# The end of a two-stage kernel as steps of its written order, and the bias of the rest rows stored twice

## The chip, the cores and the metric

The kernel runs on one core of a Trainium2 chip. The metric is the device time of one execution in microseconds (us), the median of the runs taken; each profiled execution also has a span, from its first to its last instruction.

## The reference

All numbers are float32. Stage one is attention over 8 batches (b), 8 heads, 576 tokens and a head width of 64, with a learned bias on the relative position; stage two is a soft mixture of 8 experts with 4 slots each over all 4608 tokens of width 512.

```python
scores = q @ k.T / sqrt(64)
x = log1p(abs(i - j)) / log1p(max(i, 1))
bias = relu(x[..., None] @ w1 + b1) @ w2          # hidden 32, one column per head
attn = softmax(scores + bias) @ v
x = attn as [4608, 512]                           # heads side by side
logits = x @ phi                                  # 32 slots
slot_in = softmax(logits, axis=0).T @ x           # over all tokens
slot_out[e] = relu(slot_in[e] @ w1[e]) @ w2[e]    # 512 -> 1024 -> 512
out = softmax(logits, axis=1) @ slot_out
```

## The kernel before

The work is cut into steps, and one text, `ORDER` (lines 24 to 238, 2568 steps), gives the sequence in which all steps are issued. A step is written `name/unit`, with a `+` that picks the other engine or the other form, and `@` with the PSUM banks that it takes. Each engine, and the queue of SyncE (SP) that issues nearly every transfer, goes through its own instructions in that sequence, so a transfer that waits for its buffer holds all the transfers behind it.

Attention is 40 units: 16 for the first pair of heads (two passes over the 8 batches) and 8 for each of the other three pairs. A unit has score tiles p of 128 query rows: tiles 0 to 3 are rows of one batch, and tile 4 is the 64 rest rows (576 = 4 x 128 + 64) of two batches. Per tile: `S` makes the scores on TensorE (line 519 in quarters, with a `+`, or line 513), `t` adds the bias on VectorE and keeps the extreme (530), `e` is the exponential on ScalarE (538), `a`, `m` and `n` divide (545, 549, 432), `T` and `R` turn the tile (491), `c` and `cR` copy it out of PSUM (435). Per unit, `M` multiplies by v (625), `x` copies and `xs` stores; `lq` and `lv` load q, k and v two units ahead.

The bias is made in the first hundred us, beside the first units, by 36 jobs of 16 rows each: `f` (971, 973), `B` (983), `E` (991, 993), and `D` (999), which stores the rows to memory. Jobs 0 to 31 go to `bias_m`, 128 rows for each of tiles 0 to 3; jobs 32 to 35, the 64 rest rows, go to `bias_r`. `b0` to `b4` (load_bias, line 421) read them back for a pair of heads: `b0` to `b3` in one transfer of 128 rows, `b4`, in which the 64 rows are wanted twice, in two transfers of 64 rows.

From unit 32 on, each batch is folded into the mixture's state: `K`, `KR`, `L`, `D`, `W`, `Z` on TensorE, and for the output weights `C` (turned logits), `cA`, `cB`, `cC` (826 to 834, on VectorE but for the exponential, 838). The 64 weight tiles of 512 KB come in one fixed sequence: `w0` and `w1` steps fetch 23 of them during attention, the steps from `wbm0` to `wxk` fetch 24 into buffers that attention gives back, and `r0` to `r16` fetch the last 17, each into a buffer that the first layer has used up. The first layer is `F0` to `F7` (1065), then `H`, `U`, `V` (1079, 1081, 1087, 435), in two halves Q; `k0` and `k1` turn the output weights (1111, 1114), each after the `cC` of four batches.

Behind the last step of the order stands a piece written out by hand (lines 1194 to 1216): second(cg, Q) is the second layer (1138) for a quarter cg of the output columns and a half Q of the slots; keep_second, gather (1148) and keep_gathered bring the result to the layout that the last product needs; outputs (1170) makes 512 KB halves that put copies (one on ScalarE, one on VectorE) and stores at once on SP's queue (1176); outputs_rest (1182) and put_rest do the same for the rest rows.

Of the kernel before, what the change touches and what calls it, by code (L numbers as in the profile page):

```python
# [29 lines left out]
E8/-1 f22.3/-1 D12/-1 f16.3/-1 E19/-1 f18.2/-1+ f17.0/-1 f17.3/-1 f17.2/-1 B17/-1@0 E17/-1 D10/-1  # L30
f16.0/-1 f16.2/-1 B16/-1@4 f22.2/-1+ f21.0/-1 E16/-1 f18.3/-1+ D15/-1 f22.0/-1 f23.3/-1 f18.1/-1 D8/-1
f22.1/-1 B22/-1@6 D19/-1 f23.1/-1+ f20.3/-1 D17/-1 f5.2/-1 E22/-1 D16/-1 f18.0/-1 B18/-1@2 f20.2/-1
f21.2/-1 f23.2/-1 f23.0/-1 f21.1/-1 E18/-1+ f5.1/-1 f1.2/-1 B23/-1@0 f21.3/-1+ B21/-1@4 f20.1/-1+ f20.0/-1+
B20/-1@6 E23/-1+ f3.3/-1+ S1/0+@2,0 f3.0/-1 E21/-1 f4.0/-1 E20/-1+ f3.1/-1+ f0.3/-1 b1/-1 t1.0/0
t1.1/0 S1/1+@4,6 t1.1/1 f1.0/-1+ f1.3/-1+ D22/-1 f3.2/-1+ f5.0/-1 f0.2/-1 B1/-1@2 t1.0/1 B3/-1@0
f0.1/-1 f5.3/-1+ B5/-1@6 e1.1/0 E5/-1+ e1.0/0 a1/0 D18/-1 f0.0/-1+ m1/0 f4.3/-1 f2.1/-1
f2.0/-1 D23/-1 D21/-1 B0/-1@4 E0/-1+ f4.2/-1 D20/-1 b2/-1 E3/-1 E1/-1 f2.3/-1+ f4.1/-1
S2/0+@0,6 n1.0/0 t2.1/0 lq/2 f2.2/-1+ e1.1/1 n1.1/0 t2.0/0 T1/0@2 c1/0 e2.1/0 B2/-1@4
e2.0/0 E2/-1 B4/-1@2 f7.2/-1 E4/-1+ D4/-1 a2/0+ S2/1+@6,0 m2/0 lq/3 t2.0/1 e1.0/1
e2.0/1 t2.1/1 e2.1/1 S1/2@2,4 t1.0/2 n2.0/0 n2.1/0 T2/0@6 t1.1/2 c2/0 S2/2@0,2 a2/1+  # L40
# [1231 lines left out]
```

## Time and profile before

| | |
|---|---|
| three runs | 577.73, 579.60 and 580.16 us; median 579.60 us |
| the profiled execution | 582.73 us, span 580.7 us |
| busy | TensorE 544.7 us, ScalarE 439.9, VectorE 426.7, GpSimd 230.7 |
| memory traffic | 115.92 MB |

A busy time is the merged time of an engine's instructions in the span. "PE" is the matmul side of TensorE and "PEld" its weight load, which overlaps it. "Chain" is the chain of work that ended last, followed back from the last instruction. A DMA share of 1 means that all 16 transfer engines had work.

### The profile page before, as it was taken

The numbers are of one execution on the slowest core, as the hardware profiler recorded it, in microseconds if no ns is written. First come the engines' busy times: TensorE is split into PE (matmuls) and PEld (weight loads), VectorE is DVE, ScalarE is ACT, GpSimd is POOL, SyncE is SP. The second block draws the span as 40 slices with busy tenths as digits, with TensorE's granted clock in tenths as the row PEclk, the third lists the DMA queues.
The fourth block names the chain that finished last, engine by engine and source line by source line (L and its number), as shares of the span: only waits on it lengthen the run. The fifth ranks groups of instructions, "written<-read, shape, count | busy, mean of one in ns | idle before, by whom it ended". The sixth has DMA issues, their size and how long they took to land.

```text
span 580.7 us, 23472 instructions
## 1 busy us (share of the span) xinstructions
PE 544.7 (94%) x9871; PEld 368.4 (63%) x9871; DVE 426.7 (73%) x1177; ACT 439.9 (76%) x925; POOL 230.7 (40%) x373
## 2 busy tenths in 40 slices
...
GB/s 175 294 144 185 186 284 244 168 241 228 243 142 85 171 115 196 85 245 145 84 64 140 304 189 293 128 43 217 104 181 165 181 149 307 330 323 400 152 320 333
DMA packets 46040, 115.92 MB, mean 200 GB/s; under 512 B 5488, under 2 KB 9712, under 8 KB 45936
## 3 DMA queue, kind: packets, MB, share of 16 engines
...
q10 hardware_dynamic: 144, 0.29, 0.1%
...
## 4 chain that ended last, share of the span: by engine, by line
PE 71%; DVE 11%; DMA 7%; POOL 4%; issue 3%; ACT 3%; SPq 1%; DVEq 0%; POOLq 0%; ACTq 0%
PE ps L625 18%; PE ps L519 14%; PE ps L491 14%; PE ps L513 7%; PE ps L983 5%; DVE y L530 4%; POOL y L432 3%; PE ps L1138 3%; DMA qk<-in_qk_dram 3%; PE ps L1065 3%; DVE f L973 2%; PE ps L705 2%; DMA xo<-xs 1%; PE ps L847 1%; DVE at L435 1%
## 5 line engine op out<-in xcount | busy, mean ns | idle before, releaser
L432 POOL TENSOR_SCALAR y<-y,sm 128x576 f32<-128x576 f32 x288 | 212.0, 751 | 148.0 <-DVE sm L549 91.8
L538 ACT ACTIVATE y<-y,mn 128x576 f32<-128x576 f32 x288 | 220.6, 769 | 18.1 <-DVE mn L530 12.9
L530 DVE CUSTOM_DVE_ANT_0 y<-ps,bm 128x576 f32<-128x576 f32 x256 | 185.4, 752 | 48.9 <-PE ps L519 30.6
L625 PE MATMUL ps<-at,v 64*64 64x288 f32 (+2 forms) x2880 | 163.6, 357 | 0.1
L435 ACT COPY at<-ps 128x1024 f32<-128x1024 f32 (+2 forms) x136 | 109.4, 819 | 34.3 <-PE ps L491 31.0
L519 PE MATMUL ps<-qk 64*64 64x512 f32 (+1 forms) x1600 | 124.1, 409 | 2.8 <-DVE mn L530 1.7
L625 PEld LDWEIGHTS ps<-at,v 64*64 64x64 f32 x2880 | 102.3, 133 | 24.3 <-DVE mn L530 0.2
L491 PE MATMUL ps<-ident,y 64*128 64x64 f32 x2592 | 107.7, 227 | 6.4 <-DVE mn L530 1.8
L491 PEld LDWEIGHTS ps<-ident,y 64*128 64x128 f32 x2592 | 93.9, 139 | 25.9 <-POOL y L432 9.8
L519 PEld LDWEIGHTS ps<-qk 64*64 64x64 f32 x1600 | 70.0, 132 | 62.8 <-issue 41.7
L435 DVE COPY at<-ps 128x1024 f32<-128x1024 f32 (+2 forms) x88 | 73.0, 841 | 4.7 <-PE ps L491 3.9
L513 PE MATMUL ps<-qk 64*128 64x64 f32 (+1 forms) x352 | 58.8, 436 | 0.3 <-DVE at L435 0.2
L545 POOL TENSOR_SCALAR sm<-sm 128x2 f32<-128x2 f32 x64 | 14.2, 221 | 104.5 <-ACT y L538 101.9
L538 ACT ACTIVATION_READ_ACCUMULATOR y<-y,mn 128x1 f32 x288 | 54.9, 190 | 0.0
L513 PEld LDWEIGHTS ps<-qk 64*128 64x128 f32 x352 | 39.2, 187 | 16.6 <-issue 13.0
L973 DVE TENSOR_SCALAR f<-tabs,scl,nb 128x512 f32<-128x512 f32 (+17 forms) x95 | 46.6, 547 | 1.0 <-DMA bias_m<-e 0.7
L983 PE MATMUL ps<-f,wbd 128*32 128x79 f32 (+47 forms) x640 | 41.5, 390 | 3.9 <-DVE f L973 2.5
L971 ACT ACTIVATE f<-tabs,cols,scl 128x432 f32<-128x432 f32 (+17 forms) x49 | 34.5, 752 | 3.0 <-DVE scl L335 1.8
L530 DVE CUSTOM_DVE_ANT_0 y<-ps,br 128x576 f32<-128x576 f32 x32 | 23.2, 754 | 14.9 <-PE ps L519 7.6
L983 PEld LDWEIGHTS ps<-f,wbd 128*32 128x32 f32 x640 | 20.0, 109 | 22.1 <-issue 9.5
L549 DVE RECIPROCAL sm<-sm 128x2 f32<-128x2 f32 x144 | 22.7, 162 | 10.9 <-POOL sm L545 8.2
L435 ACT COPY xts<-ps 128x576 f32<-128x576 f32 (+2 forms) x31 | 16.8, 541 | 13.8 <-PE ps L625 12.0
...
## 6 DMA issues: line engine op xcount, KB each, us to landing
wt<-in_moe_w_dram SPq DMA_DIRECT2D x62, 512.0 KB, 6.9
qk<-in_qk_dram SPq DMA_DIRECT2D x32, 576.0 KB, 4.6
v<-in_v_dram SPq DMA_DIRECT2D x40, 288.0 KB, 4.6
bias_m<-e SPq DMA_DIRECT2D x32, 295.5 KB, 3.8
bm<-bias_m SPq DMA_DIRECT2D x16, 576.0 KB, 5.4
out_dram<-ob SPq DMA_DIRECT2D x16, 512.0 KB, 4.9
...
xs<-xts SPq DMA_DIRECT2D x16, 288.0 KB, 5.3
```

The source lines that it names most:

```text
L432: nc.gpsimd.tensor_scalar(out=out, in0=y, scalar1=r, scalar2=1.0, op0=ALU.mult, op1=ALU.mult)
L435: (nc.vector.tensor_copy if eng else nc.scalar.copy)(out=out, in_=in_)
L491: nc.tensor.matmul(out, src[rs], ident[rs, rs], is_transpose=True, start=True, stop=True, tile_position=(64 * r, 0))
L513: nc.tensor.matmul(pss[hh].t[:, n, 0:w], x[rs, S + QP[p]:S + QP[p] + P], x[rs, ks], start=True, stop=True, tile_position=(64 * hh, 0))
L519: nc.tensor.matmul(pss[hh].t[64 * r:64 * r + 64, n, 0:w], x[rs, q0:q0 + 64], x[rs, ks], start=True, stop=True, tile_position=(64 * hh, 64 ...
L530: nc.vector.tensor_tensor_reduce(out=d["y", p][:, :, hh], in0=blocks(d["ps", p][hh].read().rearrange("a n j -> a (n j)")[:, 0:S]), in1=blo ...
L538: nc.scalar.activation(out=y, in_=y, func=AF.Exp, bias=d["mn", p][:, hh:hh + 1], scale=-1.0, accum_out=d["sm", p][:, hh:hh + 1])
L549: nc.vector.reciprocal(out=r, in_=r)
L625: nc.tensor.matmul(d["po"].t[64 * c:64 * c + 64, hh, 0:n], d["v"][rs, 64 * k:64 * k + 64], at[0][rs, k, c, cs], start=k == 0, stop=k == 8, ...
L971: nc.scalar.activation(out=f, in_=tabs[:, 0:n], func=AF.Relu, bias=cols[:, 1:2], scale=sc)
L973: nc.vector.tensor_scalar(out=f, in0=tabs[:, 0:n], scalar1=sc, scalar2=nb1[:, 0:1], op0=ALU.mult, op1=ALU.max)
L983: nc.tensor.matmul(pb.t[32 * t:32 * t + 32, a // 512, a % 512:a % 512 + c1 - c0], wbd, x, start=True, stop=True, tile_position=(0, 32 * t))
```

## The change

The hand-written piece is gone. Each of its calls is a step of the order now, with its copy and its store apart (`s` second, `so` keep_second, `g` gather, `ss` keep_gathered, `o` outputs, `p` copy, `P` store, `X`, `px` and `PX` for the rest rows), so that the order has 2644 steps, and they stand among the others: `s0.0` comes behind `F7` and ahead of the second half's `H`, `U`, `V`; `k1` comes behind all four of `s0.0`, `s1.0`, `s0.1` and `s1.1`; `k0`, `C/38` and `C/39` come ahead of `F0`. The whole order is another one, with other places for nearly all steps; the computation of each step is the same. Of the `w` steps 21 instead of 23 come ahead of the tail, and two (`w0/28`, `w0/27`) fetch the last two weight tiles between `s0.1` and `g0`. Of the 128 score steps with a choice 81 instead of 84 run in quarters.

The rest rows' bias goes to a fifth block of `bias_m` with 128 rows, the 64 rows twice: jobs 32 to 35 store twice, and `b4` is one transfer. The diff, with the end alone of the order:

```diff
--- before
+++ after
...
-M2/39 cB/37 d1/38 d2/38 d3/38 wy4/39 W/38@6 J1/38@3 fx/39 x/39 L/39@0 lc/39
-J2/38 J3/38 wc/38+ cB/36 wy5/39 Z/38@4 J4/38 J5/38 J6/38 wy2/39 zc/38 D/39@6
-dq/39 d1/39 F1/38 K23/39@0 wy1/39 kc23/39 K01/39@4 kc01/39+ d2/39 KR/39@0 krd/39+ W/39@4
-krc/39 F2/38@6 F3/38 wc/39 wv/39 wat/39 Z/39@7 zc/39 Tt/39@0 Tc/39 J7/38 J8/38
-F0/39@4 F1/39 F2/39 F3/39 F4/39@6 wxo/39 F5/39 F6/39 d3/39 wxk/39 wxt/39 r0/39
-r1/39 r2/39 r3/39 F7/39 r4/39 r5/39 r6/39 r7/39 cC/37 r8/39 r9/39 dq/38+
-r10/39 C/39@0 r11/39 r12/39 r13/39 cC/35 r14/39 r15/39 vs/39 H1.1/39 H1.0/39 H0.0/39
-U1/39@2 V1.1/39 V1.0/39 H0.1/39 U0/39@6 k0/39@2 kA0/39+ kB0/39 V0.0/39 V0.1/39 C/38@4 cA/38
-cB/38 cC/38 cC/36 cA/39 cB/39 cC/39 k1/39@2 kA1/39 vg/39 kB1/39 r16/39 zz/39"""
...
+cR1/39 T0/39@6 T1/39@2 wy1/39 c0/39+ cB/36 K23/38@0 kc23/38+ D/38@4 d1/38 c1/39 M0/39@6
+M1/39 M2/39 d2/38 W/38@2 d3/38 C/37@0 cA/37 vg/39 x/39 J1/38@5 J2/38 fx/39
+L/39@6 wc/38+ cC/34 Z/38@0 zc/38 lc/39 D/39@2 dq/39 J3/38 J4/38 d1/39 J5/38
+wy4/39 F1/38 K23/39@6 kc23/39 K01/39@0 d2/39 wv/39 KR/39@6 krc/39 J6/38 J7/38 wat/39
+kc01/39+ W/39@2 dq/38+ C/38@0 krd/39+ F2/38@4 wxt/39 wc/39 Z/39@6 F3/38 C/39@2 zc/39
+Tt/39@4 Tc/39 cA/38 k0/39@6 wxo/39 F0/39@0 wxk/39 r0/39 r1/39 r2/39 r3/39 F1/39
+F2/39 cC/36 r4/39 r5/39 r6/39 r7/39 r8/39 r9/39 r10/39 r11/39 cA/39 cB/38
+F3/39 r12/39 F4/39@2 cB/39 J8/38 d3/39 vs/39 kA0/39+ r13/39 r14/39 r15/39 r16/39
+H0.1/39 H0.0/39 U0/39@4 F5/39 F6/39 cC/38 F7/39 V0.1/39 V0.0/39 s0.0/39@0 H1.1/39 H1.0/39
+U1/39@4 V1.0/39 s1.0/39@1 V1.1/39 s0.1/39 so0/39+ w0/28 kB0/39 s1.1/39 w0/27 cC/39 g0/39@0
+cB/37 cC/37 k1/39@2 kB1/39 so1/39 g1/39@1 ss1/39 ss0/39+ o0.0/39@4,6 p0.0.1/39 P0.0.1/39 kA1/39+
+o0.1/39@0,2 p0.1.0/39 p0.0.0/39+ s2.0/39@6 P0.0.0/39 s2.1/39 p0.1.1/39+ P0.1.1/39 so2/39+ P0.1.0/39 X0/39@4,0 px0.0/39+
+px0.1/39 PX0/39 o1.1/39@2,6 p1.1.1/39+ p1.1.0/39 P1.1.0/39 o1.0/39@0,4 P1.1.1/39 p1.0.0/39 g2/39@2 ss2/39 p1.0.1/39+
+X1/39@6,0 o2.0/39@2,4 p2.0.1/39 px1.0/39+ px1.1/39+ P1.0.0/39 PX1/39 P1.0.1/39 o2.1/39@6,0 p2.0.0/39+ P2.0.0/39 p2.1.1/39
+p2.1.0/39+ s3.0/39@4 P2.1.0/39 P2.0.1/39 s3.1/39 X2/39@2,0 px2.1/39+ so3/39+ g3/39@5 ss3/39 o3.0/39@6,0 P2.1.1/39
+px2.0/39+ p3.0.0/39+ PX2/39 p3.0.1/39 P3.0.1/39 X3/39@4,2 px3.0/39+ px3.1/39+ PX3/39 P3.0.0/39 o3.1/39@0,6 p3.1.0/39
+P3.1.0/39 p3.1.1/39+ P3.1.1/39 zz/39"""
...
@@ -317,8 +324,7 @@
     stS = const.tile([P, 1], F32, name="stS")
 
 
-    bias_m = dram.tile([4, P, H, S + P], F32, name="bias_m")
-    bias_r = dram.tile([64, H, S + 64], F32, name="bias_r")
+    bias_m = dram.tile([5, P, H, S + P], F32, name="bias_m")
     xs = dram.tile([B, NP - 1, P, S], F32, name="xs")
 
 
@@ -376,9 +382,9 @@
     for c in range(5):
         for m in range(8 if c < 4 else 4):
             bases = [P * c + 16 * m + 4 * t for t in range(4)]
-            dst = bias_m[c, 16 * m:16 * m + 16] if c < 4 else bias_r[16 * m:16 * m + 16]
-            jobs.append((bases, [4 * len(jobs) + t for t in range(4)],
-                         dst[:, :, (112 if c < 4 else 48) - 16 * m:][:, :, 0:S + 15].rearrange("p h j -> (p h) j")))
+            dsts = [bias_m[c, 16 * n:16 * n + 16, :, 112 - 16 * n:127 - 16 * n + S].rearrange("p h j -> (p h) j")
+                    for n in ((m,) if c < 4 else (m, m + 4))]
+            jobs.append((bases, [4 * len(jobs) + t for t in range(4)], dsts))
 
     units = [(0, b, k) for k in (1, 2) for b in range(B)] + [(hp, b, 0) for hp in range(1, NP) for b in range(B)]
     U = len(units)
@@ -421,11 +427,9 @@
     def load_bias(hp, c):
         if c < 4:
             x = bsp.tile([P, 2 * S], F32, name="bm", tag="bm")
-            read_bias(x, bias_m[c], 2 * hp)
         else:
             x = bsp.tile([P, 2 * S], F32, name="br", tag="br", bufs=1)
-            for r in range(2):
-                read_bias(x[64 * r:64 * r + 64], bias_r, 2 * hp)
+        read_bias(x, bias_m[c], 2 * hp)
         biases[hp][c] = x
 
     def norm(out, y, r):
@@ -957,7 +961,7 @@
 
     def bias_job(i):
 
-        bases, scales, dst = jobs[i]
+        bases, scales, dsts = jobs[i]
         n = max(bases[0] + 16, S - bases[0])
         i0 = bases[0] + 16
         o0 = 512 - i0 if 0 <= 512 - i0 and S + 15 - i0 <= 512 else 0
@@ -996,7 +1000,12 @@
             step(-1, f"f{i}.{t}", lambda eng, t=t: feats(eng, t))
         step(-1, f"B{i}", products)
         step(-1, f"E{i}", keep)
-        step(-1, f"D{i}", lambda _: nc.sync.dma_start(out=dst, in_=d["e"]))
+
+        def put_rows(_):
+            for dst in dsts:
+                nc.sync.dma_start(out=dst, in_=d["e"])
+
+        step(-1, f"D{i}", put_rows)
 
     def warm(_):
         for _ in range(11):
@@ -1170,10 +1179,12 @@
             nc.tensor.matmul(hs[r // 2].t[:, r % 2], ends["ss"][rs, cg], ends["cT", q][rs], start=True, stop=True,
                              tile_position=(32 * r, 0))
 
-    def put(eng, cg, q, z):
-        x = ob()
-        cp(eng, x, ends["O", cg, q][z].read())
-        nc.sync.dma_start(out=out[cg, q, z].rearrange("p (x d) -> p x d", x=2), in_=x)
+    def keep_outputs(eng, cg, q, z):
+        ends["ob", cg, q, z] = ob()
+        cp(eng, ends["ob", cg, q, z], ends["O", cg, q][z].read())
+
+    def put(cg, q, z):
+        nc.sync.dma_start(out=out[cg, q, z].rearrange("p (x d) -> p x d", x=2), in_=ends["ob", cg, q, z])
 
     def outputs_rest(cg):
         hs = ends["X", cg] = Banks(2), Banks(2)
@@ -1182,38 +1193,33 @@
             nc.tensor.matmul(hs[r // 2].t[:, r % 2, 0:P], ends["ss"][rs, cg], small()[rs, 1], start=True, stop=True,
                              tile_position=(32 * r, 0))
 
+    def keep_rest_outputs(eng, cg, z):
+        if ("obr", cg) not in ends:
+            ends["obr", cg] = ob()[:, 0].rearrange("a (r n) -> a r n", r=4)
+        cp(eng, ends["obr", cg][:, 2 * z:2 * z + 2], ends["X", cg][z].read()[:, :, 0:P])
+
     def put_rest(cg):
-        x = ob()[:, 0].rearrange("a (r n) -> a r n", r=4)
+        nc.sync.dma_start(out=outr[cg].rearrange("p (r n) -> p r n", r=4), in_=ends["obr", cg])
+
+    for cg in range(4):
+        for Q in range(2):
+            step(V, f"s{cg}.{Q}", lambda _, cg=cg, Q=Q: second(cg, Q))
+        step(V, f"so{cg}", lambda eng, cg=cg: keep_second(not eng, cg))
+        step(V, f"g{cg}", lambda _, cg=cg: gather(cg))
+        step(V, f"ss{cg}", lambda eng, cg=cg: keep_gathered(eng, cg))
+        for q in range(2):
+            step(V, f"o{cg}.{q}", lambda _, cg=cg, q=q: outputs(cg, q))
+            for z in range(2):
+                step(V, f"p{cg}.{q}.{z}", lambda eng, cg=cg, q=q, z=z: keep_outputs(eng, cg, q, z))
+                step(V, f"P{cg}.{q}.{z}", lambda _, cg=cg, q=q, z=z: put(cg, q, z))
+        step(V, f"X{cg}", lambda _, cg=cg: outputs_rest(cg))
         for z in range(2):
-            cp(z, x[:, 2 * z:2 * z + 2], ends["X", cg][z].read()[:, :, 0:P])
-        nc.sync.dma_start(out=outr[cg].rearrange("p (r n) -> p r n", r=4), in_=x)
+            step(V, f"px{cg}.{z}", lambda eng, cg=cg, z=z: keep_rest_outputs(eng, cg, z))
+        step(V, f"PX{cg}", lambda _, cg=cg: put_rest(cg))
 
     with tc.manual_schedule():
         for _, _, f in sorted(prog, key=lambda x: x[:2]):
             f()
-        second(0, 0)
-        second(0, 1)
-        keep_second(1, 0)
-        second(1, 0)
-        gather(0)
-        keep_gathered(0, 0)
-        for cg in range(4):
-            if cg < 3:
-                second(cg + 1, 1)
-                keep_second(1, cg + 1)
-            outputs(cg, 0)
-            put(0, cg, 0, 0)
-            put(1, cg, 0, 1)
-            outputs(cg, 1)
-            put(0, cg, 1, 0)
-            put(1, cg, 1, 1)
-            if cg < 3:
-                gather(cg + 1)
-                keep_gathered(0, cg + 1)
-                if cg < 2:
-                    second(cg + 2, 0)
-            outputs_rest(cg)
-            put_rest(cg)
 
 
 def _tables():
```

## Rows read from the trace of the kernel before

**Rows 1.** The page: busy time, share and instructions of each engine.
```profile
PE 544.7 (94%) x9871; PEld 368.4 (63%) x9871; DVE 426.7 (73%) x1177; ACT 439.9 (76%) x925; POOL 230.7 (40%) x373
```

**Rows 2.** Busy time by stretch: stretch, length, engines (instructions), granted clock, DMA share, GB/s.
```profile
500.00:510.00 10.00, 8.43 (x152) 4.65 (x148) 5.39 (x13) 4.84 (x10) 0.29 (x1) 1.00 1.03 405
...
sum 500.00, PE 483.36 PEld 333.06 DVE 397.95 ACT 420.72 POOL 230.43; mean PE 9.67 PEld 6.66 DVE 7.96 ACT 8.41 POOL 4.61
```

**Rows 3.** TensorE in order of time: start, us, line, count, [idle before, releaser].
```profile
514.15 15.49 PE L1065 MATMUL ps<-wt,sT 128*32 128x512 f32 x128
...
532.62 0.66 PE L1087 MATMUL ps<-ident,hS 128*128 128x128 f32 x4 [1.01 <-DVE hS L1081]
...
538.30 0.90 PE L1111 MATMUL ps<-ident,ck 128*128 128x128 f32 x3 [4.07 <-DVE ck L834]
540.40 0.48 PE L1111 MATMUL ps<-ident,ck 128*128 128x128 f32 x1 [1.21 <-DVE ck L834]
```

**Rows 4.** The chain that ended last, from 541 us: start, us, engine and line.
```profile
541.25 7.04 PE ps L1138 x192
...
548.70 1.89 PE ps L1138 x64
550.59 1.08 PE ps L1170 x8
...
552.75 0.49 PE ps L1148 x2
```

**Rows 5.** Busy time by stretch, around the gap on TensorE.
```profile
529.64:534.20 4.56, 3.55 (x36) 2.80 (x36) 2.47 (x4) 1.32 (x4) 0.00 (x0) 1.00 1.02 411
...
538.30:541.25 2.95, 1.74 (x16) 0.95 (x20) 1.51 (x6) 0.61 (x2) 0.00 (x0) 0.50 1.01 400
...
545.00:546.00 1.00, 1.00 (x47) 1.00 (x40) 0.00 (x0) 0.00 (x0) 0.00 (x0) 1.00 0.08 16
```

**Rows 6.** SP's queue in order of time, from 517 us: start, us, transfers issued.
```profile
517.64 16.68 SPq L953 DMA_DIRECT2D wt<-in_moe_w_dram  x17
552.73 2.88 SPq L1176 DMA_DIRECT2D out_dram<-ob  x4
...
575.24 1.15 SPq L1189 DMA_DIRECT2D out_dram<-ob  x1
```

**Rows 7.** Busy time by stretch, cut where weights and stores begin and end.
```profile
500.00:552.70 52.70, 43.97 (x655) 23.68 (x647) 18.07 (x53) 10.60 (x24) 0.29 (x1) 0.87 0.80 303
552.70:580.70 28.00, 17.41 (x342) 11.70 (x342) 10.66 (x14) 8.57 (x15) 0.00 (x0) 0.90 0.87 338
...
541.60:552.70 11.10, 10.91 (x273) 8.82 (x262) 1.53 (x3) 1.35 (x4) 0.00 (x0) 0.86 0.09 36
```

**Rows 8.** Transfers by line: count, KB each, us from issue to landing.
```profile
bm<-bias_m SPq DMA_DIRECT2D x16, 576.0 KB, 5.4
out_dram<-ob SPq DMA_DIRECT2D x16, 512.0 KB, 4.9
...
br<-bias_r SPq DMA_DIRECT2D x8, 288.0 KB, 5.0
```

**Rows 9.** The chain that ended last, around the rest rows' bias.
```profile
93.92 5.12 DMA bias_r<-e
...
99.84 4.75 DMA br<-bias_r
```

**Rows 10.** Busy time by stretch, in attention.
```profile
80.00:90.00 10.00, 10.00 (x200) 6.80 (x192) 9.29 (x21) 9.50 (x19) 3.14 (x5) 1.00 0.90 286
...
100.00:110.00 10.00, 8.45 (x230) 6.49 (x222) 6.14 (x22) 7.28 (x18) 4.81 (x8) 1.00 0.66 167
...
150.00:160.00 10.00, 8.67 (x176) 6.04 (x166) 7.80 (x21) 6.74 (x15) 4.79 (x7) 1.00 0.93 250
```

**Rows 11.** The page: the costliest groups, both forms of the scores on TensorE.
```profile
L519 PE MATMUL ps<-qk 64*64 64x512 f32 (+1 forms) x1600 | 124.1, 409 | 2.8 <-DVE mn L530 1.7
...
L513 PE MATMUL ps<-qk 64*128 64x64 f32 (+1 forms) x352 | 58.8, 436 | 0.3 <-DVE at L435 0.2
```

More of the change, by code (lines that the diff above doesn't have):

```diff
@@ L30 @@
[L30 to L40, printed above, removed]
@@ new lines @@
+f0.1/-1 f5.3/-1+ e1.0/0 e1.1/0 t1.1/1 f2.0/-1 D17/-1 B5/-1@0 a1/0 m1/0 E5/-1+ f0.0/-1+
+f4.2/-1 B0/-1@2 E0/-1+ E1/-1 f2.3/-1+ f2.1/-1 f4.0/-1 S2/0@6,0 E3/-1 f2.2/-1+ f4.1/-1 D20/-1
+b2/-1 f4.3/-1 e1.1/1 t2.1/0 lq/2 t2.0/0 n1.0/0 n1.1/0 T1/0@4 c1/0 B2/-1@2 E2/-1
+B4/-1@4 E4/-1+ e2.1/0 S2/1@0,2 lq/3 e2.0/0 a2/0+ m2/0 e1.0/1 n2.1/0 t2.0/1 t2.1/1
+a1/1+ S1/2@6,4 t1.1/2 f7.3/-1+ e2.0/1 n2.0/0 D0/-1 e2.1/1 a2/1 f7.2/-1 t1.0/2 m2/1
+T2/0@0 c2/0 S2/2@2,4 f7.0/-1 m1/1 t2.1/2 e1.0/2 f30.3/-1 f27.3/-1 R2/0@6 t2.0/2 cR2/0
```

392 lines of the change are left out of this document (198 added, 194 removed).

## The prediction

> **What bounds the kernel now.** I read the busy times first: TensorE is busy for 544.7 of 580.7 us, and ScalarE, next, for 439.9 [rows 1]. So the time is TensorE's work, plus the 36 us in which it doesn't work, plus what it loses at a lower clock. The second view is busy time by stretch, which says where the 36 us are: 16.6 before 500 us, 1.6 from 500 to 510 [rows 2], the rest behind that. The third is TensorE in order of time with its waits. Behind the first layer it waits 1.01 us for the second half's `H` on VectorE, and then, in the middle of `k1`, 4.07 and 1.21 us for the `cC` of the last batches [rows 3]. `k1` stands ahead of the second layer on TensorE, so 192 matmuls that need nothing of it wait too. The chain of waits then goes through TensorE to the last outputs [rows 4]. The granted clock is the fourth thing to see: it is 0.50 after the long wait, which is the level of 1.2 GHz, and back at 1.00 in the stretch from 545 us [rows 5]. The fifth is the queue of transfers. The last 17 weight tiles are issued up to 534.3 us, the first store at 552.73, the last at 575.24 [rows 6], and between 541.6 and 552.7 the transfer engines are busy for 9% [rows 7]. So the kernel ends with a stream of stores that cannot start before TensorE has its first output, while the transfers idle for some ten us in front of it.
>
> **The end as steps of the order.** The stretch to cost is from `F0`'s start, 514.15 us [rows 3], to the end of the first outputs, 551.67 (1.08 us from 550.59 [rows 4]).
>
> The waits go: `H`, `U`, `V` of the second half get `s0.0` and `s1.0` beside them, 1.89 us each, and `k1` stands behind four second-layer steps and one `g`. That is 1.01 + 4.07 + 1.21 = 6.29 us [rows 3]. What hides the rest of `cC` now is 4 x 1.89 = 7.6 us of second layer, and the last layer-one steps ahead of it. What is late next is the last of these, `cC/37`: its exponential stands on ScalarE behind `so0` and `kB0`, so it can't begin before `s0.1` has ended. One batch's share of that work sets the distance of the two late parts of `k1`, 540.40 - 538.30 = 2.1 us [rows 3]; `s1.1` and `g0` lie beside it, 1.89 and at most 0.49 [rows 4], so it is just covered, and if not, it costs a few tenths.
>
> The low clock goes with the gap: the three second-layer steps from 541.25 took 7.04 us, at full clock three take 3 x 1.89 = 5.67 [rows 4], 1.37 us saved. Against this a second `g` now stands ahead of the first outputs, at most 0.49 [rows 4].
>
> `k0`, `C/38` and `C/39` move ahead of `F0`. From 529.64 to 534.20 TensorE is busy for 3.55 us [rows 5]; 16 of the 36 matmuls there are the turns of `U`, of which four took 0.66 [rows 3], so at most 2.64, and at least 0.9 us is what moves. TensorE idles 1.57 us from 500 to 510 [rows 2], where the chain of the last batch has gaps, so between none and all of the 0.9 is hidden. I take 0.6 as gained, since the gaps are longer than the work.
>
> Sum: 6.29 + 1.37 - 0.49 + 0.6 = 7.8 us; the first outputs would end at 543.9 and the first store be issued at 544.9.
>
> **The stream of stores.** Before, it takes 28.0 us from 552.7 to the end, for 9.46 MB at 338 GB/s; the weights went at 405 and 411 [rows 2, 5, 7]. At 405 it would take 23.4 us. Splitting copies from stores and setting `s2` and `s3` at other places lets the queue be filled more evenly, so the bounds are 0 and 4.6 us gained. But two weight tiles more come in the tail, 2 x 0.524 MB, 2.6 us at 405. The weights were in by about 542.6 (0.4 MB came in 541.6 to 552.7 [rows 7]), so now by 545.2, and the first stores queue behind them for some tenths. On SP's queue the stores stand behind these two fetches, which wait for buffers of the first layer; that is done some ten us before. A seventh output buffer may have to wait for an early store to land, 4.9 us [rows 8], at a time when the queue is full anyway. I take 0 for all of it together, from -3 (gain) to +1.
>
> **The rest rows' bias.** Four more stores of 295.5 KB, 1.21 MB, fall where transfers are at a share of 0.90 and 286 GB/s [rows 10]: 4.2 us of transfer time. The path is the last job's store, 5.12 us, and then the read, landed at 104.6 us [rows 9]; TensorE idles 1.55 us from 100 to 110 [rows 10]. The read becomes one transfer of 576 KB, which lands in 5.4 us, where the halves take 5.0 [rows 8]. The trace has no double store. Its bounds are a gain of 1.55 (the idle time gone) and a loss of 4.2 (all of it on the path). I take +0.4, the difference of the two landings, which is the nearest row, since most of the extra bytes go out before the last job.
>
> **The order elsewhere.** Three score steps leave the quarters: 124.1 / 100 steps is 1.24 us each, 58.8 / 44 is 1.34 [rows 11], so +0.3. Copies change between ScalarE and VectorE, with 141 and 154 us to spare each [rows 1], so 0. The two moved fetches free 1 MB of transfers in attention: 0. What the new sequence does to TensorE's 16.6 idle us before 500 can't be read from this trace. Single stalls there cost 1.33 and 1.55 us, in 150 to 160 and in 100 to 110 [rows 10]; I take 0, with two such stalls fewer (-2.9) and four more (+5.5) as ends.
>
> **Sum.** -7.8 + 0 + 0.4 + 0.3 + 0 = -7.1 us, span 573.6. The profiled execution of before took 582.73 us, 2.03 outside its span, and is 3.1 above the median of the runs; the gain is taken from the median: 579.6 - 7.1 = 572.5 us.
>
> **Rivals.**
> (a) *The transfers bind.* From 500 us on, 303 x 52.7 and 338 x 28.0 make 25.4 MB [rows 7], with the two tiles 26.5 MB. If weights and stores, now side by side, go at the stores' 338 GB/s, they end at 578.3, and the gain is 2.4: 577.2 us. For it speaks the share of 0.87 in the store stretch, which is near full; against it that 405 to 411 were reached [rows 2, 5]. I give it 0.08. The Trainium skill (DMA: Bandwidth & Descriptors, section Where 436 GB/s comes from) puts the limit for one core's transfers between memory and SBUF at about 358 GB/s; the trace disagrees, with 411. By that figure the 26.5 MB would end at an estimated 574 us.
> (b) *Attention gives it back.* Four to seven more stalls of 1.33 to 1.55 us: 577 to 582 us. For it: nearly every step has a new place, and nothing in this trace vouches for it. Against it: TensorE idles only 3.3% before 500 us, the steps still have two units of lead for q, k and v. 0.10.
> (c) *The change doesn't do what it says.* `k1` still waits, because the `cC` of the last four batches stand in VectorE's queue behind copies that wait for the second layer. The gap of 5.28 us comes back just ahead of the first outputs: 577.8 us. 0.04.
> (d) *Slower.* SP's queue is the mechanism: the bias and weight transfers of attention stand at new places in it, and each one that comes in front of a unit's q and k when TensorE needs them costs a stall of the kind in 150 to 160, 1.33 us, where transfers were at a share of 0.93 [rows 10]. To be slower by 0.5% it must come in 8 units more than now (7.1 + 2.9 = 10.0 us), in 12 of the 38 units with such loads it gives 572.5 + 16 = 588. 0.06.
> (e) *Attention gains as well*, by two stalls or more, or the stream runs at 405: below 567.5. 0.10.
>
> **How the numbers follow.** The forecast has 0.62, with 568 to 576.7 as its own spread (the bounds of the hidden turns, of the stores and of the bias). A measurement tells about 0.5% from no change, which is 576.7 to 582.5. Faster is the forecast, (e), and a little of (a): 0.75; same is the rest of (a), (b) and (c): 0.19; slower is (d): 0.06. The range that leaves out two in ten goes from 567.0, in (e), to 578.0, past (a) and (c).
>
> **What would show it.** Right: between `F0` and the first outputs TensorE has no wait of over 1 us and the clock stays at 1.00; that stretch is some 29.5 us long, where it was 37.5; the first store is issued within 31 us of `F0`'s start, with weights landing until then; the store stream takes 25 to 28 us; `F0` begins at 514 to 515. Wrong: `F0` begins late (attention, then (b) or (d)); the idle time before 500 us is far from 16.6; `k1` or the first outputs wait for VectorE, (c); the stores run at 338 or less from a full queue, (a); the read of the rest rows lands later than 105 us and TensorE waits for it.

## The result and the profile after

| | before | after |
|---|---|---|
| median of the runs | 579.88 us (577.73 to 582.22) | 573.58 us (572.24 to 575.42) |
| ratio | 1 | 0.9893, 95% interval 0.9845 to 0.9940 |
| the profiled execution, span | 582.73, 580.7 us | 573.29, 571.5 us |
| `F0`'s start | 514.15 us | 515.86 us |
| from there to the first store | 38.58 us | 28.44 us |
| first store to the end | 28.0 us | 27.2 us |

The kernel became 6.3 us faster; 7.1 were forecast. The two spans differ by 9.2 us, since the profiled execution of before was slower than all four of its runs. They split into three: +1.7 up to `F0`, -10.1 in the end that was rewritten, -0.8 in the stream of stores.

The page and busy time by stretch (stretch, length, busy time of TensorE's matmul side, its weight load, VectorE, ScalarE, GpSimd with instructions, granted clock, DMA share, GB/s), for [rows 1, 2, 5, 7]:

```profile
PE 538.3 (94%) x9847; PEld 374.3 (65%) x9847; DVE 432.6 (76%) x1186; ACT 434.1 (76%) x913; POOL 238.7 (42%) x376
...
0.00:500.00 500.00, 480.52 (x8819) 339.03 (x8823) 402.02 (x1113) 414.74 (x874) 238.36 (x374) 1.00 0.54 181
515.93:529.94 14.01, 14.01 (x132) 4.63 (x135) 4.85 (x16) 1.61 (x3) 0.00 (x0) 1.00 1.02 391
540.19:544.30 4.11, 2.66 (x24) 1.16 (x23) 1.65 (x2) 1.51 (x4) 0.00 (x0) 1.00 0.89 353
544.30:571.50 27.20, 16.96 (x340) 12.06 (x340) 10.91 (x15) 8.12 (x12) 0.00 (x0) 0.89 0.90 351
```

TensorE idles 19.5 us before 500 us, where it idled 16.6, but from `F0` to the first store its clock is at 1.00 throughout, and the transfer engines, at a share of 0.09 in the 11 us ahead of the first store before [rows 7], are at 0.89 in the last four now. TensorE in order of time through the end, for [rows 3]:

```profile
512.98 1.41 PE L860 MATMUL ps<-xk,ek 128*32 128x128 f32 x40
...
515.86 8.79 PE L1074 MATMUL ps<-wt,sT 128*32 128x512 f32 x80
524.58 1.09 PE L1096 MATMUL ps<-ident,hS 128*128 128x128 f32 x8
525.60 5.36 PE L1074 MATMUL ps<-wt,sT 128*32 128x512 f32 x48
530.78 1.93 PE L1147 MATMUL ps<-wt,hT 128*32 128x128 f32 x64
532.64 1.09 PE L1096 MATMUL ps<-ident,hS 128*128 128x128 f32 x8
533.66 5.45 PE L1147 MATMUL ps<-wt,hT 128*32 128x128 f32 x192
539.04 0.49 PE L1157 MATMUL ps<-so,small 128*128 128x128 f32 x2
539.36 0.60 PE L1120 MATMUL ps<-ident,ck 128*128 128x128 f32 x4
539.89 0.30 PE L1123 MATMUL ps<-ident,ck 64*32 64x64 f32 x2
541.35 0.31 PE L1123 MATMUL ps<-ident,ck 64*32 64x64 f32 x6 [1.16 <-issue]
```

The second layer (line 1147) runs ahead of `k1` (1120, 1123), as the order says, and no matmul waits for VectorE. The first layer takes 14.15 us where it took 15.49. One wait is new: 1.16 us in the middle of `k1`, put down to "issue", that is, to nothing that the profile shows. SP's queue, for [rows 6]:

```profile
512.04 23.86 SPq L957 DMA_DIRECT2D wt<-in_moe_w_dram  x22
544.30 2.88 SPq L1187 DMA_DIRECT2D out_dram<-ob  x4
...
562.81 2.94 SPq L1187 DMA_DIRECT2D out_dram<-ob  x3
```

### The profile page after: what moved, and what is told of

Its sections match the earlier page's. It is cut to its first block, busy times and chain, and to the rows that moved or that the text cites. A ratio compares the mean times of both kernels' runs of the same rounds, so it can differ in the third digit from the quotient of the medians.

```text
span 571.5 us, 23414 instructions
## 1 busy us (share of the span) xinstructions
PE 538.3 (94%) x9847; PEld 374.3 (65%) x9847; DVE 432.6 (76%) x1186; ACT 434.1 (76%) x913; POOL 238.7 (42%) x376
## 3 DMA queue, kind: packets, MB, share of 16 engines
q8 instruction: 77, 1.26, 0.9%
## 4 chain that ended last, share of the span: by engine, by line
PE 72%; DVE 10%; DMA 6%; ACT 5%; issue 3%; POOL 3%; DVEq 0%; POOLq 0%; SPq 0%; ACTq 0%
PE ps L629 20%; PE ps L523 15%; PE ps L495 14%; PE ps L517 6%; PE ps L987 4%; DVE y L534 4%; DVE f L977 3%; POOL y L436 3%; PE ps L1147 3%; DMA xo<-xs 3%; PE ps L1074 2%; DMA v<-in_v_dram 2%; ACT y L542 2%; PE ps L709 2%; DMA qk<-in_qk_dram 1%
## 5 line engine op out<-in xcount | busy, mean ns | idle before, releaser
L523 PE MATMUL ps<-qk 64*64 64x512 f32 (+1 forms) x1552 | 119.7, 408 | 5.6 <-DMA qk<-in_qk_dram 2.4
L629 PEld LDWEIGHTS ps<-at,v 64*64 64x64 f32 x2880 | 103.8, 133 | 24.8 <-ACT at L439 1.2
L523 PEld LDWEIGHTS ps<-qk 64*64 64x64 f32 x1552 | 71.2, 133 | 58.5 <-issue 37.4
L439 DVE COPY at<-ps 128x256 f32<-128x256 f32 (+2 forms) x85 | 72.4, 858 | 8.0 <-PE ps L495 6.4
L517 PE MATMUL ps<-qk 64*128 64x512 f32 (+1 forms) x376 | 61.6, 436 | 0.2 <-DVE at L439 0.2
L517 PEld LDWEIGHTS ps<-qk 64*128 64x128 f32 x376 | 42.3, 187 | 17.5 <-issue 12.5
L977 DVE TENSOR_SCALAR f<-tabs,scl,nb 128x400 f32<-128x400 f32 (+17 forms) x95 | 44.5, 523 | 1.6 <-ACT e L997 1.2
L987 PE MATMUL ps<-f,wbd 128*32 128x79 f32 (+48 forms) x640 | 41.4, 390 | 3.1 <-DVE f L977 2.4
L975 ACT ACTIVATE f<-tabs,cols,scl 128x368 f32<-128x368 f32 (+17 forms) x49 | 34.3, 748 | 3.2 <-DVE scl L341 1.8
L439 ACT COPY xts<-ps 128x576 f32<-128x576 f32 (+2 forms) x27 | 14.9, 550 | 15.2 <-PE ps L629 13.9
```

Of the source, the lines that this page charges most:

```text
L439: (nc.vector.tensor_copy if eng else nc.scalar.copy)(out=out, in_=in_)
L517: nc.tensor.matmul(pss[hh].t[:, n, 0:w], x[rs, S + QP[p]:S + QP[p] + P], x[rs, ks], start=True, stop=True, tile_position=(64 * hh, 0))
L523: nc.tensor.matmul(pss[hh].t[64 * r:64 * r + 64, n, 0:w], x[rs, q0:q0 + 64], x[rs, ks], start=True, stop=True, tile_position=(64 * hh, 64 ...
L629: nc.tensor.matmul(d["po"].t[64 * c:64 * c + 64, hh, 0:n], d["v"][rs, 64 * k:64 * k + 64], at[0][rs, k, c, cs], start=k == 0, stop=k == 8, ...
L975: nc.scalar.activation(out=f, in_=tabs[:, 0:n], func=AF.Relu, bias=cols[:, 1:2], scale=sc)
L977: nc.vector.tensor_scalar(out=f, in0=tabs[:, 0:n], scalar1=sc, scalar2=nb1[:, 0:1], op0=ALU.mult, op1=ALU.max)
```

## The experiments

"Old" means the kernel before with one thing of the change, "new" the kernel after with one thing undone; ratios are to the kernel before, run beside each.

| kernel | median us (range) | ratio, 95% interval | `F0`, first store, end of the profiled run |
|---|---|---|---|
| tail_old | 573.64 (571.16 to 574.87) | 0.9896 (0.985 to 0.994) | 513.21, 543.10, 570.6 |
| hand_new | 579.56 (578.02 to 580.89) | 1.0002 (0.998 to 1.003) | 516.09, 548.26, 576.2 |
| twice_old | 578.52 (576.64 to 581.91) | 0.9986 (0.996 to 1.001) | 512.22, 550.26, 577.9 |
| once_new | 572.78 (571.30 to 575.83) | 0.9888 (0.985 to 0.993) | 515.30, 543.75, 571.0 |
| k1_old | 576.09 (573.34 to 579.22) | 0.9932 (0.990 to 0.996) | 511.29, 547.08, 574.8 |
| warm_old | 579.15 (575.57 to 581.84) | 0.9984 (0.995 to 1.001) | 511.75, 548.15, 576.2 |
| cC_early | 574.83 (573.57 to 576.18) | 0.9914 (0.988 to 0.995) | 517.72, 546.35, 573.7 |
| w_early | 576.26 (572.08 to 578.77) | 0.9937 (0.991 to 0.996) | 520.34, 549.68, 576.9 |
| eight_less | 572.45 (569.93 to 580.48) | 0.9864 (0.982 to 0.990) | 516.88, 543.88, 571.2 |
| half_stores | 570.68 (569.29 to 572.56) | 0.9845 (0.981 to 0.988) | 517.69, 546.18, 569.3 |
| tail_old_twice | 572.53 (570.48 to 576.03) | 0.9878 (0.984 to 0.992) | 515.00, 546.88, 574.2 |
| filled_twice | 571.14 (570.88 to 572.09) | 0.9839 (0.979 to 0.989) | 512.27, 541.98, 569.3 |

### Which part brings the gain

**tail_old**, before's attention and bias, and only the end as in after:

```diff
 (the kernel after, but bias_m and bias_r as before)
-(after's order up to Z/39)
+(before's order up to Z/39, with 23 w steps)
 ... Tt/39@4 Tc/39 cA/38 k0/39@6 wxo/39 F0/39@0 ... (the end of after, without w0/28, w0/27, cB/37, J8/38)
```

> The order of before up to the first layer, the rest rows' bias as before, and only the end from C/38 on as in the changed kernel (the second layer, k1 and the outputs as steps; all 23 weight tiles still fetched in attention). Theory, the end alone is the gain, and the new order of attention costs some 2 us (F0 began at 515.9 us where it began at 514.2): 7.5 to 10 us under before, 570 to 572.5, and under the changed kernel. Rival, the new attention order carries part of the gain: 3 to 6 us under before. By the trace: first outputs 8 to 10 us earlier, F0 at 514 to 515.

**hand_new**, after's attention and bias, and the end in the sequence that was written out by hand:

```diff
 (the kernel after)
-... V0.1/39 V0.0/39 s0.0/39@0 H1.1/39 ... s1.1/39 w0/27 cC/39 g0/39@0 cB/37 cC/37 k1/39@2 ...
+... V0.1/39 V0.0/39 H1.1/39 ... cC/37 k1/39@2 kB1/39 kA1/39+ s0.0/39 s0.1/39 so0/39 s1.0/39 g0/39 ss0/39 ...
```

> The changed kernel with the end back in the old sequence: k1 ahead of the second layer, then second, gather and outputs as they were written by hand; attention, bias and weight fetches as changed. Theory: the end is worth 8 to 10 us, so 7 to 10 us above the changed kernel and 0 to 3 above before. Rival, attention carries part: 3 to 5 above the changed kernel. The new sequence ahead of F0 (k0, C/38, C/39) stays, so some of the clock loss may stay away: then about 6.

By the medians the end from `C/38` on gives all of it, and the new attention with the old end gives nothing. In tail_old's profile the new end takes 29.89 us from `F0` to the first store, in hand_new's the old end takes 32.17, with `k1` waiting for VectorE again:

```profile
535.55 0.90 PE L1120 MATMUL ps<-ident,ck 128*128 128x128 f32 x3 [2.72 <-DVE ck L838]
```

That is 6.4 us less than in before: hand_new keeps `k0`, `C/38`, `C/39` and the first `cC` steps where the change put them, its first layer takes 14.15 us, and the wait for `cC` is 2.72 us and not 4.07 and 1.21. The medians don't show these 6.4: `F0` begins 1.9 us later, and the profiled run of hand_new is the fastest of its twelve, that of before slower than all of its four.

**twice_old**, the kernel before with the rest rows' bias stored twice, and **once_new**, the kernel after with it stored once:

```diff
-    bias_m = dram.tile([4, P, H, S + P], F32, name="bias_m")
-    bias_r = dram.tile([64, H, S + 64], F32, name="bias_r")
+    bias_m = dram.tile([5, P, H, S + P], F32, name="bias_m")
...
-            for r in range(2):
-                read_bias(x[64 * r:64 * r + 64], bias_r, 2 * hp)
+        read_bias(x, bias_m[c], 2 * hp)
```

> Before, with the rest rows' bias stored twice and read in one transfer, nothing else. Theory: +0.4 us, between -1 and +1.5. Rival, the 4.2 us of extra transfer time lie on the path: +3 to +4. Rival, the single read frees the stall of unit 8: -1.5.

> The changed kernel with the rest rows' bias stored once and read in two transfers of 64 rows. Theory: the same within 1 us (573 to 574.5). Rival, the doubled stores of the last three jobs hold up the q and k of unit 9 (TensorE waits 2.36 us for them at 102 us): 1.5 to 2.4 us faster.

Neither pair tells the double store from nothing: -1.3 us by the one, +0.8 by the other, and the first interval holds 1. The read lands in 4.7 us, where the forecast had 5.4 and each of the two halves took 5.0 [rows 8]; the row of after, with its count and KB:

```profile
br<-bias_m SPq DMA_DIRECT2D x4, 576.0 KB, 4.7
```

The second rival of once_new's expectation shows in the traces and not in the time: at 102 us after waits 2.36 us for q and k, once_new 0.6 us, but once_new loses 2.27 us to another wait, at 83.72 us, where after loses 1.26.

### What the pieces of the end are worth

**k1_old**, the kernel before with `k1` alone moved behind four steps of second layer:

```diff
-cB/38 cC/38 cC/36 cA/39 cB/39 cC/39 k1/39@2 kA1/39 vg/39 kB1/39 r16/39 zz/39"""
+cB/38 cC/38 cC/36 cA/39 cB/39 cC/39 vg/39 r16/39 zz/39"""
...
                 keep_second(1, cg + 1)
+            if cg == 0:
+                stack(1)
+                keep_stack(1, 1)
+                cp(0, small()[:, 1, 64:128], ends["K", 1].read()[:, 1, 0:64])
```

> Before, with k1 and its two copies alone moved: behind the second layer's fourth step, ahead of the first outputs; all else as before, written by hand. Theory: the waits of 4.07 and 1.21 us and the half clock behind them (1.37) go, so 5 to 6.6 us faster, most of the change's gain. Rival, the gain needs the second half's H, U, V beside the second layer too, or the wait comes back ahead of the first outputs: 2 us or less.

By the ratio it brings 3.9 us and not the 6.65 of the forecast's terms. The waits for `cC` are gone, but a new wait stands in the second layer itself, and the low clock behind it (76 matmuls in 4.04 us, where 64 take 1.95):

```profile
531.87 3.47 PE L1140 MATMUL ps<-wt,hT 128*32 128x128 f32 x116 [0.56 <-ACT hT L435]
537.75 4.04 PE L1140 MATMUL ps<-wt,hT 128*32 128x128 f32 x76 [2.42 <-issue]
541.73 0.49 PE L1150 MATMUL ps<-so,small 128*128 128x128 f32 x2
```

**warm_old**, the kernel before with matmuls of no use in `k1`'s two waits:

```diff
         for i in range(4):
+            for _ in range((18, 0, 0, 6)[i] if q else 0):
+                nc.tensor.matmul(h.t[:, 1, P:2 * P], ident, ident, start=True, stop=True)
             nc.tensor.transpose(out=h.t[:, 0, i * P:(i + 1) * P], in_=ck[:, 4 * q + i, 1:5]...
```

> The kernel before with 24 matmuls more that write to an unused part of k1's bank: 18 in front of k1's first turn and 6 in front of its last, in the 4.07 and 1.21 us that TensorE waits there; nothing that follows needs them. If the prediction's term for the low clock holds (1.37 us), the granted clock stays at 1.00 from 534 to 549 us, the 192 second-layer matmuls take 5.7 instead of 7.1 us, the first store is issued 1.4 to 1.9 us sooner after F0's start than the 38.58 of before, and the time falls by as much: 577.9 to 578.4 against 579.9. If the low clock costs nothing by itself, or the added matmuls run past the wait (at 0.2 us each they fill 3.6 of 4.07 and 1.2 of 1.21 us), there is no gain, 579.9 or up to 1 us more.

```profile
531.64 4.29 PE L1112 MATMUL ps<-ident 128*128 128x128 f32 x36
...
538.26 5.45 PE L1140 MATMUL ps<-wt,hT 128*32 128x128 f32 x192
```

The 192 matmuls in before:

```profile
541.18 7.11 PE L1138 MATMUL ps<-wt,hT 128*32 128x128 f32 x192
```

Each added matmul stands in the trace as two, so the 36 are the 18. With the wait filled the granted clock stays at 1.00 up to 548 us, and the 192 matmuls take 5.45 us, where before they took 7.11. `F0` to first store falls by 2.2 us (0.25 of it in the first layer). So the low clock behind the wait is caused by the wait, and in the trace it is worth 1.66 us on these matmuls, where the forecast had 1.37. In the time, 0.9 us less with an interval of -2.7 to +0.8 holds that, and holds nothing as well.

### The new wait of TensorE

Three theories: VectorE's `cC/37` is late (rival (c)); two late weight fetches are to blame; TensorE's own instructions come late while the transfer engines are full.

**cC_early**, after with the exponential and division of batch 37 earlier:

```diff
-... cC/39 g0/39@0 cB/37 cC/37 k1/39@2 ...
+(cB/37 right behind cB/39, cC/37 right behind cC/38)
```

> The changed kernel with the last batch's cB/37 and cC/37 ahead of so0 on ScalarE and VectorE, so that k1 has its operands some 3 us earlier. In the changed kernel TensorE stands still for 1.16 us within k1, at 540.2 us. Theory A, it waits for cC/37: the wait goes, and 0.5 to 1.2 us with it. Theory B, it waits for its own instructions, which come through the transfer engines while these are full: the wait of 1 to 1.3 us stays, the time is the same.

**w_early**, after with the last two fetches in attention, as before:

```diff
-... s0.1/39 so0/39+ w0/28 kB0/39 s1.1/39 w0/27 cC/39 ...
+... lv/38 w0/28 w0/27 ... (some 457 us)
```

> The changed kernel with the two late weight fetches (w0/28, w0/27) put behind the last load of v, at some 457 us, where the transfer engines stand still for 10 us; so 23 tiles come ahead of the tail as before. Theory, from the first weight tile of the tail to the last store the transfers are full and bind: 2 x 1.3 us less work for them, 1 to 2.6 us faster. Rival, TensorE still binds: the same within 0.5 us.

**eight_less**, after with 56 of the 64 weight tiles; the last quarter of the second layer uses the tiles of the quarter before, so part of the computation is changed:

```diff
             w, e, c = worder[i]
             homeof.append(home)
+            if i >= 56:
+                wtiles[i] = wtiles[i - 8]
+                continue
```

> The changed kernel without the fetch of the last eight weight tiles; the last quarter of the columns is multiplied with the tiles of the quarter before. 4.2 MB less, 10 us of transfers, so these have room from about 530 us on. Theory B of the wait at 540 us (instructions come late while the transfer engines are full): it shrinks under 0.3 us. Theory A (cC/37): it stays. The end: if the transfers bind, the stores start on an empty queue and the kernel ends 2 to 3.5 us earlier, then bound by TensorE's outputs (last copy at 564.2 us, less the wait, and 5 us of landing); if TensorE binds now, only the wait's 1.2 us.

In the first two the wait stays (1.35 and 1.19 us, in the same place), in the third it is gone. The rows of cC_early and of eight_less, and the stretch around it in eight_less, where the DMA share is 0.02:

```profile
543.39 0.31 PE L1123 MATMUL ps<-ident,ck 64*32 64x64 f32 x6 [1.35 <-issue]
```

```profile
540.92 0.32 PE L1126 MATMUL ps<-ident,ck 64*32 64x64 f32 x8
...
535.00:540.00 5.00, 5.00 (x189) 4.86 (x180) 2.14 (x9) 0.62 (x3) 0.00 (x0) 1.00 0.02 6
```

So VectorE is not the cause, and the two fetches are not. What is left can be seen in the transfers themselves. A queue of its own ("q8 instruction") brings packets of 16 KB; the transfers of after from 538.93 to 540.04 us have one, among 117 of the weights:

```profile
q1 hardware_dynamic: 117, 0.43, 98.1%
q8 instruction: 1, 0.02, 6.2%
```

I set the end of the last such packet ahead of each wait beside the time at which TensorE goes on:

| kernel | packet's end | TensorE goes on | between |
|---|---|---|---|
| after | 540.04 | 541.35 | 1.31 |
| tail_old | 537.32 | 538.72 | 1.40 |
| k1_old | 536.32 | 537.75 | 1.43 |
| cC_early | 542.02 | 543.39 | 1.37 |
| w_early | 545.32 | 546.73 | 1.41 |
| once_new | 539.34 | 540.79 | 1.45 |
| half_stores | 541.72 | 543.22 | 1.50 |
| tail_old_twice | 540.99 | 542.50 | 1.51 |
| filled_twice | 535.76 | 537.17 | 1.41 |

Nine waits in two different instructions, and each ends 1.31 to 1.51 us behind a packet. In eight_less the packet ended at 538.59, and 538.59 + 1.4 lies ahead of the matmul at 540.92. The packets are not slower under load (1.11 us in after, 1.27 in eight_less): they start later, 5.1 us behind the one before in after, 2.7 us in eight_less.

Counting shows what they hold. The 14 traces (before, after and the twelve) put 24 waits of TensorE of over 0.25 us down to "issue". Ahead of each of them stand a multiple of 256 records of TensorE (matmuls, weight loads and the few of its sequencer) and 193 or 194 more, and that multiple is the number of packets that have landed: 74 x 256 + 193 = 19137 records and 74 packets in after's end, 73 x 256 + 193 = 18881 and 73 in k1_old's. So each packet is the next 256 instructions of TensorE. At none of the 1071 such places in the 14 traces does TensorE go on sooner than 1.25 us behind the packet.

The same count shows when a packet starts. From 30 us on, where the transfer engines had been at a share of 0.02 or less for two us (278 packets), it starts 0.2 us (median) behind the first instruction of the block of 256 ahead of it; where they had been at over 0.95 (356 packets), 2.4 us. For the wait in after it is 3.38 us, in k1_old 4.68, at the same place in eight_less 0.74. So the full queue holds the packet back, and where TensorE is through a block soon (535.55 to 540.19 us in after), it waits.

w_early saves nothing in the end: its stream takes 27.2 us as well. In its profiled run the mixture's state waits 1.9 us for `xo`, where after waits 1.06, and the clock falls to 0.90 from 500 to 510 us.

### What bounds the stream of stores

**half_stores**, after, with only the first half of each 512 KB output tile stored, so half of the main output is left out:

```diff
-        nc.sync.dma_start(out=out[cg, q, z].rearrange("p (x d) -> p x d", x=2), in_=ends["ob", cg, q, z])
+        nc.sync.dma_start(out=out[cg, q, z].rearrange("p (x d) -> p x d", x=2)[:, 0:1], in_=ends["ob", cg, q, z][:, 0:1])
```

> The kernel after, with only the first half of each 512 KB output tile stored, so half of the main output is left out (4.2 of 8.4 MB); all else is the same. It tells what the 27.2 us from the first store to the end are made of. If the transfers bind them, the end comes with the last product: the last copy ended at 564.2 us in after, 19.9 us behind the first store, and a 256 KB store lands in 5.0 us, so the stretch is some 22 to 25 us and the time 569 to 571.5. If TensorE's chain of second layer, gather, outputs and copies binds, the stretch stays within 1 us of 27.2 and the time at 573.6 less at most 1. A stretch of 20 or less would say that copies waited for buffers that stores held.

```profile
546.18:569.30 23.12, 16.97 (x340) 12.05 (x340) 10.90 (x15) 8.10 (x12) 0.00 (x0) 0.93 0.62 229
```

The stream shrinks from 27.2 to 23.1 us. The last copy ends 19.9 us behind the first store in both, so not the bytes but the chain of second layer, gather, outputs and copies sets 19.9, and the bytes stored at least 4.1 of the 7.3 us behind it. The late weights have no part in it: in eight_less, which issues its last at 525.8 us, the stream takes 27.3 us.

### The clock ahead of the first layer

**tail_old_twice**, tail_old with the double store, meant to be the best of the parts:

```diff
 (tail_old)
+(bias_m with five blocks, as in after)
```

> The kernel before with the new end and the rest rows' bias stored twice, but with the attention order of before. The end alone gave 573.64, the double store alone 578.52 against 579.79. If the parts add up and the double store is worth what the two pairs showed (between -1.3 and +0.8 us, both intervals with 0 in them), this lands at 572.3 to 574.4, and no verdict over the kernel after. If the new attention order is what costs 3 us at F0, F0 begins at 511 to 513.5 us here, as in the kernels with the old order, where the kernels with the new one have 515.3 to 517.7.

Its median is no other than after's. But its profiled run shows what tail_old's, whose order is the same around `F0`, doesn't: the first rows are tail_old's, the others its own.

```profile
508.61 0.49 PE L498 MATMUL ps<-ident,et 64*128 64x64 f32 x5 [0.97 <-ACT xk L442]
...
510.26 1.41 PE L863 MATMUL ps<-xk,ek 128*32 128x128 f32 x40
...
513.21 8.79 PE L1072 MATMUL ps<-wt,sT 128*32 128x512 f32 x80
...
512.00:519.00 7.00, 6.86 (x71) 2.52 (x73) 3.52 (x14) 0.88 (x3) 0.00 (x0) 1.00 0.95 364
```

```profile
508.19 0.69 PE L495 MATMUL ps<-ident,et 64*128 64x64 f32 x5 [0.98 <-ACT xk L439]
...
510.23 2.50 PE L860 MATMUL ps<-xk,ek 128*32 128x128 f32 x40
...
515.00 10.51 PE L1074 MATMUL ps<-wt,sT 128*32 128x512 f32 x80
...
512.00:519.00 7.00, 7.00 (x54) 3.00 (x54) 3.65 (x14) 0.84 (x3) 0.00 (x0) 0.53 0.59 213
```

One sequence, with nearly the same waits ahead of it (0.60, 0.97 and 0.62 us in tail_old, 0.60, 0.98 and 0.42 here), and once the clock stays at 1.00, once it is at its lower level for ten us. The two spans differ by 3.6 us. In five of the six profiled runs with before's attention and nothing in these waits (before, twice_old, k1_old, warm_old, tail_old_twice) the 40 matmuls take 2.4 to 2.5 us, in tail_old 1.41; in all seven with after's attention, whose waits there are other ones, 1.41.

**filled_twice**, tail_old_twice with seven matmuls of no use in the three waits ahead of `F0`:

```diff
-... KR/39@0 krd/39+ W/39@4 krc/39 dq/38+ C/38@0 ...
+... wm1/39 KR/39@0 krd/39+ wm2/39 W/39@4 krc/39 dq/38+ wm3/39 C/38@0 ...
...
+    def fill(n):
+        for _ in range(n):
+            nc.tensor.matmul(psa[:, 3, 0:P], ident, ident, start=True, stop=True)
+
+    step(V, "wm1", lambda _: fill(2))
+    step(V, "wm2", lambda _: fill(4))
+    step(V, "wm3", lambda _: fill(1))
```

> tail_old_twice with 7 matmuls more into an unused bank, in the three waits of TensorE ahead of the first layer (0.60 us before the turns of KR: 2; 0.98 us before those of W: 4; 0.42 us before those of C/38: 1; at 0.24 us each). In tail_old_twice's profile the granted clock fell to 0.50 from 508.5 to 518.5 us behind these waits, and the stretch from there to F0's end took 3.6 us more than in tail_old's, whose order is the same there and whose clock stayed at 1.00. If the waits are what lets the clock fall, it stays at 1.00 here, the 40 matmuls ahead of F0 take 1.41 instead of 2.50 us and the first layer 8.79 + 5.36; the time is 570.5 to 572.5 with less spread, against 572.53 for tail_old_twice. If the clock falls for another reason, the profile shows 2.4 to 2.5 us for the 40 and 10.5 for the 80 in some of the runs' times still, and the median stays at 572.5 or is some tenths above it.

```profile
506.63 1.16 PE L1206 MATMUL ps<-ident 128*128 128x128 f32 x8
...
509.33 1.41 PE L860 MATMUL ps<-xk,ek 128*32 128x128 f32 x40
...
512.27 8.79 PE L1074 MATMUL ps<-wt,sT 128*32 128x512 f32 x80
...
512.00:519.00 7.00, 7.00 (x73) 2.25 (x76) 2.62 (x11) 0.58 (x2) 0.00 (x0) 1.00 1.02 384
```

Of the kernels that do all of the work this has the lowest median, 571.14 us, and its six runs lie within 1.2 us, where those of tail_old_twice lie within 5.6. The mean granted clock of a whole run is 0.993 to 0.996 in all six. Of the twelve runs of tail_old and tail_old_twice, the five with 0.984 to 0.987 took 574.07 to 576.03 us, the seven with 0.990 to 0.994 took 570.48 to 573.20. The intervals of the two ratios overlap, so the 1.4 us between the medians is not told by them; the spread is. Why one execution of the same order keeps the clock and another does not stays open.

## Why the prediction was right

**The end as steps.** Forecast -7.8, measured -10.1 from `F0` to the first store. Right: the waits for `H` and `cC`, 6.29 us, are gone; the low clock behind them is gone (warm_old); the second layer covers the rest of `cC`. "So it is just covered" was right for `cC/37`: it ends on VectorE at 539.25 us, `k1` starts at 539.36, and no wait for VectorE is left. Wrong: "between `F0` and the first outputs TensorE has no wait of over 1 us". There is one of 1.16 us, where rival (c) put one, but not by its cause. The forecast had no term for it. In before a packet ended at 537.26, inside the 4.07 us [rows 3] and some 8 us ahead of its first instruction, and the second layer ran with the transfer engines at 0.09 [rows 7]; now it runs while the weights come.

Four sizes were too small. The rows of before for them, the first a stretch with its granted clock of 0.77:

```profile
515.00:520.00 5.00, 5.00 (x40) 1.30 (x36) 2.13 (x10) 0.00 (x0) 0.00 (x0) 0.77 0.94 344
...
529.57 0.52 PE L491 MATMUL ps<-ident,lp 64*128 64x64 f32 x5
...
533.12 0.60 PE L1111 MATMUL ps<-ident,ck 128*128 128x128 f32 x4
533.65 0.32 PE L1114 MATMUL ps<-ident,ck 64*32 64x64 f32 x8
533.89 0.33 PE L491 MATMUL ps<-ident,lq 64*128 64x64 f32 x3
```

The low clock of [rows 5] cost the 192 matmuls 1.66 us and not 1.37, and it also lay on `k1`'s own turns, 0.90 + 0.48 + 0.44 us against 0.60 + 0.32 now: 0.9. The moved turns were put at 0.6; what left the stretch is `k0`, 0.77 us from 533.12 to 533.89, and the turns of `C/39` and `C/38`, 0.45 and 0.33: 1.55. And [rows 3] gave the first layer at 15.49 us; I took that for its length, though it too held a stretch at the lower clock: 14.15 now, 1.34 less. I had looked for the clock behind the gap, and not ahead of it. Together, with the new wait and the second `g`: 6.29 + 1.66 + 0.9 + 1.55 + 1.34 - 1.16 - 0.49 = 10.1, all that was measured; the busy times overlap, so the tenths are rough.

**The order elsewhere.** Forecast 0, between -2.9 and +5.5. TensorE idles 2.8 us more before 500 us in after than in before, and it is no accident of one run: its busy time up to there is 483.4 to 485.0 us in the seven profiled kernels with before's attention and 478.8 to 481.2 in the seven with after's. So rival (b) holds in its mechanism, with two or three stalls' worth instead of its four to seven. Most of it is waits for the transfers of q, k and v, 3.5 us in after where before has 0.6. Waits of TensorE in after (us in total, times, the longest):

```profile
PE ps L523 <- DMA qk<-in_qk_dram: 2.4, 1, 2.4
...
PE ps L629 <- DMA v<-in_v_dram: 1.1, 2, 0.9
```

In the seven kernels with after's attention these waits come to 2.2 to 4.3 us, in the seven with before's to 2.0 at most. The instruction wait is there as well, at one place of the new order: 1.26 us in after, ending at 81.19, 1.41 us behind a packet that ended at 79.78; the same in the six others, with 1.29 to 1.47 us. It is paid back in part around `F0`, by the clock and the turns' place: `F0` starts only 1.7 us later. What the search gained in attention is nothing that can be measured: tail_old against after, hand_new against before.

**The stream of stores.** Forecast 0, measured -0.8, and 27.2 lies in the 25 to 28 that was named. Rival (a) fails: the weights came at 391 GB/s, nearly all of them ahead of the first store, and the stores went at 351, where it had 338 for both. The Trainium skill (DMA: Bandwidth & Descriptors, section Where 436 GB/s comes from) puts the limit of one core's transfers between memory and SBUF at about 358 GB/s. By the row of 515.93 to 529.94 us the measurement disagrees, with 391. But half_stores shows what "I take 0 for all of it together" left open: 4.1 us of the stream hang on the stores' bytes, the rest on TensorE's chain and its copies.

**The bias.** Forecast +0.4; nothing measurable. The upper bound, +4.2, is refused by twice_old (at most +0.8); the lower, -1.55, is not.

**SP's queue**, rival (d): its mechanism is seen, in the waits for q, k and v above, with some 3 us more and not the 10 to 16 that would have made the kernel slower. The two fetches that moved behind `s0.1` were put at 0. w_early has a median 2.7 us above after's, but the intervals of the two ratios overlap; it stays open whether they are worth anything where they are now.

**The sum.** By the spans -9.2 against -7.1, by the medians -6.3. That the total came so close is partly luck: the end was put 2.3 us too small, and the order elsewhere, put at 0, lost some of that again. `F0` begins at 511.29 to 515.00 us in the seven kernels with before's attention and at 515.30 to 520.34 in the seven with after's. That the gain was taken from the median and not from the profiled execution was right: before's runs go from 573.0 us of span at a mean clock of 0.990 to 585.4 at 0.975, and its profiled run had 0.984.
